# Part 1's mixture in 18 chunks of 256 tokens at 192 bytes from the weights, not 12 blocks of 384

## The chip, the core and the metric

The kernel runs on one core of a Trainium2 chip. The metric is the device time of one execution in microseconds (us). The engines are named as the profile names them: PE (TensorE matmuls), PEld (TensorE's weight loads, which overlap PE), DVE (VectorE), ACT (ScalarE), POOL (GpSimd) and SP, whose queue issues most DMAs.

## The reference, cut to what matters

```python
B, H, S, D = 8, 8, 576, 64                      # attention; keys and values pooled by 8
k_p = k.reshape(B, H, S // 8, 8, D).mean(axis=3)
v_p = v.reshape(B, H, S // 8, 8, D).mean(axis=3)
attn = softmax(q @ k_p^T / sqrt(D))             # 72 scores for each token and head
x = (attn @ v_p).transpose(0, 2, 1, 3).reshape(4608, 512)
# Part 1's mixture, d_ff 768
h = np.maximum(np.maximum(x @ w1, x @ w2), x @ w3)
y = h @ w_out                                   # (4608, 512)
# Part 2, d_ff 2048
z = np.maximum(y @ w_in, 0.0)
out = z * z @ w_out2
```

All is float32. Each matmul operand is split in a high and a low half (`PARTS`: high·high, high·low, low·high), so one product of 128x128 weights takes three matmuls.

## The kernel before

**Part 1** takes 4608 tokens in 12 blocks of 384 (`T1`, `NB1`). `attention(j)` makes the x of block j, and `moe1(j)` the mixture on it. `moe1` is a generator of 22 steps (`STEPS`): for each of the 6 slices f of d_ff three steps e, each a group of 12 matmuls into one PSUM tile `ps` (three such tiles in `mm_ps`, shared by all steps); e = 0 is copied by ACT to `hm` (L547), e = 1 and 2 are joined by DVE's max (L549), and after e = 2 `split` makes h, the high half on ACT (L135) and the low on DVE (L136). Then come four output steps d, each a group of 18 matmuls over the six h, copied by ACT to `ys` (L566) and stored by a DMA from ACT's queue to `y_dram` (L567). `x` lies in eight buffers, h in six, two more (`ah_p`) serve the first two slices of block 1.

**The order** is written out by hand. Every load, softmax, transpose, value product and mixture step is put in `todo` with a due time, in units of one step; `run` sorts them. Step i of block j is due at `j * STEPS + i`; the first six steps of block 1 are due among the output steps of block 0. Attention for block j is due about one block ahead, spread by `pace`. The weights of Part 1 are converted from 64 bit to two float32 halves on the chip (`convert`, `split`) during the first steps, and those of Part 2 (`load_second`, `prepare_in`, `prepare_out`) between block 2 and the last block (`SECOND`), with results parked in DRAM; the second of each pair of arrays combines rows first (L478, L507, four DVE operations).

**Placement.** The pools stand one behind another in SBUF: `const`, `w_p` (weights of Part 1), `x_p`, `h_p`, `t_p` from the left. A weight array is 4096 bytes for each partition, an x or h tile 3072, all multiples of 256, so x and h start at the same place as the weights modulo 256. `ah_p` lies elsewhere, at 128 modulo 256 from them. In Part 2 `leave(y_p, 192)` and two more such calls put the moving operand 192 bytes from the stationary one modulo 256, in both of its products.

**Part 2** takes 9 blocks of 512 tokens with matmuls of 128x256 (L701, L825), and reads y back from `y_dram` (`load_y`, L644), piecewise where a half of 256 tokens crosses a block of 384.

Of the kernel before, what the change touches and what calls it, by code (L numbers as in the profile page):

```python
# [32 lines left out]
NE = 3  # L33
T1 = 384
NB1 = NT // T1
T2 = 512
NB2 = NT // T2

# [4 lines left out]


STEPS = NE * KF1 + KD

# [15 lines left out]
AHEAD = 2  # L64
BRISK = 0.7

SECOND = (2, NB1 - 1)


NATURAL = 1  # L70
# [25 lines left out]
def attention_moe_kernel(ctx: ExitStack, tc: tile.TileContext, q, k, v, vn, w1, w2, w3, wo1, wi2, wo2, out):  # L96
# [20 lines left out]
        (m, g, h): dram.tile([P, 2, 2, 256], F32, name=f"wo2_dram{m}_{g}_{h}")  # L117
        for m in range(1, 8) for g in range(2) for h in range(2)
    }
    y_dram = [dram.tile([KD, P, T1], F32, name=f"y_dram{j}") for j in range(NB1)]  # L120

# [55 lines left out]


    w_p = s1.enter_context(tc.tile_pool(name="w_p", bufs=1))
    x_p = s1.enter_context(tc.tile_pool(name="x_p", bufs=2 * KD))
    h_p = s1.enter_context(tc.tile_pool(name="h_p", bufs=KF1))
    t_p = s1.enter_context(tc.tile_pool(name="t_p", bufs=2))

    s_at = ctx.enter_context(ExitStack())
# [2 lines left out]
    sm_p = s_at.enter_context(tc.tile_pool(name="sm_p", bufs=4, side="right"))  # L189
    pt_p = s_at.enter_context(tc.tile_pool(name="pt_p", bufs=2, side="right"))  # L190
    xf_p = s_at.enter_context(tc.tile_pool(name="xf_p", bufs=1, side="right"))
    ah_p = s_at.enter_context(tc.tile_pool(name="ah_p", bufs=AHEAD, side="right"))
    sc_ps = s_at.enter_context(tc.tile_pool(name="sc_ps", bufs=2, space=PSUM))
    tr_ps = s_at.enter_context(tc.tile_pool(name="tr_ps", bufs=1, space=PSUM))
    av_ps = s_at.enter_context(tc.tile_pool(name="av_ps", bufs=1, space=PSUM))
# [8 lines left out]
    kbd = kv_p.tile([P, NPAIR, 2, SP], F32, name="kbd")  # L204
    nc.gpsimd.memset(kbd, 0.0)
    vst_f = []
    for _ in range(2):
        vf = t_p.tile([P, T1], F32, tag="ys", name="vst_f")[:SP].rearrange("s (p a d) -> s p a d", a=3, d=D)
        nc.gpsimd.memset(vf, 0.0)
        vst_f.append(vf)  # L210
    K_SCALE = 1.0 / (POOL * D**0.5)
# [80 lines left out]

    def attention(j):

        x_t[j] = [None] * NPAIR
        n_tiles = sum(NPAIR * len(score_tiles(n)) for _, _, n, _ in pieces(j))
        pace = (STEPS - 1) / n_tiles
        at = (j - 1) * STEPS + pace / 2 - (LAG_T + LAG_V + LEAD_X)
        brisk = BRISK if j == 1 else 1
        pace *= brisk  # L300
        if j > CARRIED and j % 3 == 1:
            at -= 1
            pace *= 0.88
        for b, s0, n, t in pieces(j):
            if s0 == 0 and b < NATURAL:
                tiles = []
                when = at - pace / 2 + LAG_T + LAG_V if t else at + pace / 2
                todo.append((when - LEAD_LOAD, lambda b=b, tiles=tiles: tiles.extend(load_natural(b))))
                todo.append((when, lambda tiles=tiles: pool_v(tiles)))
            for p in range(NPAIR):  # L310
                load, prepare, softmax, carry, transpose, values = attend(j, b, s0, n, p, t)
                todo.append((at - brisk * LEAD_LOAD, load))
                todo.append((at - brisk * LEAD_PREP, prepare))
                todo.append((at, softmax))
                late = 0
                if j >= CARRIED:
                    todo.append((at + LAG_C, carry))
                    late = 1
                todo.append((at + brisk * LAG_T + late, transpose))
                at += pace * len(score_tiles(n))  # L320
                todo.append((at - pace + brisk * (LAG_T + LAG_V) + late, values))
# [10 lines left out]
    def attend(j, b, s0, n, p, t):  # L332
# [56 lines left out]
        def transpose():  # L389
# [12 lines left out]
            for h in range(2):  # L402
# [13 lines left out]
                else:  # L416
                    nc.scalar.activation(pt[0][:, h, :n], tr, AF.Copy)

        def values():
            if t == 0:  # L420
                x_t[j][p] = x_p.tile([P, 2, T1], F32R, tag="x", name="x")
            x = x_t[j][p][:, :, t : t + n]
            if whole:
                av = av_ps.tile([P, T1], F32, tag="av0", name="av0")[:, :n]
                for h in range(2):
                    nc.tensor.matmul(
                        av, lhsT=vst_f[p // 2][:, p % 2, h : h + 2].rearrange("p a d -> p (a d)"), rhs=pt[0][:, h, :n],
                        start=(h == 0), stop=(h == 1),
                    )
                split(x, av)  # L430
                return
            hi, lo = pt[0][:, 0, :, :n], pt[0][:, 1, :, :n]
            xf = xf_p.tile([P, T1], F32, tag="xf", name="xf")[:, :n]
            for h in range(2):
                av = av_ps.tile([P, T1], F32, tag=f"av{h}", name=f"av{h}")[:, :n]
                lhsT = vst[:, p, 2 * h : 2 * h + 2].rearrange("p a d -> p (a d)")
                nc.tensor.matmul(av, lhsT=lhsT, rhs=hi[:, h], start=True, stop=False)  # L437
                nc.tensor.matmul(av, lhsT=lhsT, rhs=lo[:, h], start=False, stop=True)  # L438
                r, o = slice(h * D, (h + 1) * D), slice((1 - h) * D, (2 - h) * D)
                nc.scalar.activation(xf[r], av[o], AF.Copy)  # L440
                nc.vector.tensor_tensor(out=xf[r], in0=av[r], in1=xf[r], op=ALU.add)  # L441
            split(x, xf)

        return load, prepare, softmax, carry, transpose, values

# [82 lines left out]

    def moe1(j):

        x = x_t.pop(j)
        hs = []
        for f in range(KF1):
            hm = t_p.tile([P, T1], F32, tag="hm", name="hm")
            h = (ah_p if j == 1 and f < AHEAD else h_p).tile([P, 2, T1], F32R, tag="h", name="h")
            for e in range(NE):
                ps = mm_ps.tile([P, T1], F32, tag="ps", name="ps")
                n = 0
                for kk in range(KD):
                    for a, c in PARTS:  # L540
# [12 lines left out]
            hs.append(h)  # L553
            now[0] = hm
        for d in range(KD):
            ps = mm_ps.tile([P, T1], F32, tag="ps", name="ps")
            n = 0
            for kk in range(KF1):
                for a, c in PARTS:
                    nc.tensor.matmul(  # L560
                        ps, lhsT=wo1_t[kk][:, a, d * P : (d + 1) * P], rhs=hs[kk][:, c],
                        start=(n == 0), stop=(n == 3 * KF1 - 1),
                    )
                    n += 1
            ys = t_p.tile([P, T1], F32, tag="ys", name="ys")
            nc.scalar.activation(ys, ps, AF.Copy)  # L566
            nc.scalar.dma_start(out=y_dram[j][d], in_=ys)  # L567
            yield
# [6 lines left out]
    def add_moe1(j):  # L575
        steps = moe1(j)
        for i in range(STEPS):
            when = j * STEPS + i
            if j == 1 and i < NE * AHEAD:
                when = NE * KF1 + i * KD / (NE * AHEAD)  # L580
            todo.append((when, functools.partial(next, steps, None)))

    todo = []
# [3 lines left out]
            todo.append((0.9 * (NE * f + e) - 12, functools.partial(load_w1, f, e)))  # L587
    for kk in range(KF1):
        todo.append((0.9 * (NE * KF1 + kk) - 12, functools.partial(load_wo1, kk)))
    for j in range(NB1 - 1):  # L590
        add_moe1(j)
        attention(j + 1)

    second = []
    for f in range(0, KF2, 2):
# [39 lines left out]
    def load_y(j):  # L635

        for n, (r, h) in enumerate(((0, 0), (0, 1), (1, 0), (1, 1))):
            yr = shared_place(n, [P, 2, HT], "yr")
            for i in range(2):
                t = 0  # L640
                while t < HT:
                    b, o = divmod(j * T2 + h * HT + t, T1)
                    n = min(HT - t, T1 - o)
                    nc.sync.dma_start(out=yr[:, i, t : t + n], in_=y_dram[b][2 * r + i, :, o : o + n])  # L644
                    t += n
            yr_t[j, r, h] = yr

    def mix_y(j):
# [30 lines left out]
    early.append(functools.partial(fetch_in, 0, w2_p))  # L679
    early += [functools.partial(split_y, 0, m) for m in ORDER]  # L680
    for i, f in enumerate(early):
        todo.append(((NB1 - 1) * STEPS + (i + 0.5) * (NE * KF1) / len(early), f))
    add_moe1(NB1 - 1)
    run()
    s1.close()
    g_p = ctx.enter_context(tc.tile_pool(name="g_p", bufs=4, reuse_waits="tile"))
# [214 lines left out]
```

## Time and profile before

| | |
|---|---|
| time, median of 3 runs | 1459.99 us (1458.57 to 1462.32) |
| the profiled execution's own time | 1462.14 us |
| its span in the trace | 1459.7 us |
| Part 1's last matmul, Part 2's first | 749.3 us |
| PE, PEld busy | 98%, 96% of the span |
| DVE, ACT, POOL busy | 67%, 52%, 13% |

The span is what the trace covers, from the first instruction to the last; the execution's own time is 2.4 us longer. Busy shares are means over stages that differ, so a stage is read by itself.

### The profile page before, as it was taken

The page shows a single profiled execution, that of the slowest core. Times are in us where ns is not written, and L with a number is a line of the kernel's source. Part 1 is how long each engine was busy: PE and PEld are TensorE (multiplying, and loading weights), DVE is VectorE, ACT ScalarE, POOL GpSimd, SP SyncE. Part 2 cuts the span into 40 slices and gives each one's busy share as a digit, 9 for nine tenths or more (in the row PEclk, how much of TensorE's full clock was granted, in tenths as well). Part 3 has the DMA queues.
Part 4 walks back from the last instruction along what each step waited for, and adds up shares of the span by engine and source line. Part 5 has one row for each costly group of instructions (what it writes and reads, how often), then busy time and mean ns, then how long its engine had stood idle before and what let it go on. Part 6 is the DMA issues. An engine that isn't in the chain of part 4 may idle for free.

```text
span 1459.7 us, 27670 instructions
## 1 busy us (share of the span) xinstructions
PE 1425.5 (98%) x10410; PEld 1403.0 (96%) x10410; DVE 977.9 (67%) x1754; ACT 759.4 (52%) x1959; POOL 182.9 (13%) x229
## 2 busy tenths in 40 slices
PE   6889999999999999999999999999999999999998
PEld 4879999999999999999999999999999999999998
DVE  5887477656675756646336767686867767686865
ACT  7795366655665657655223544453535444454543
POOL 3441022212322222221000000000000000000000
PEclk9989999999999999999999999999999999999999
DMA  7554145444455444433459747566566666555746
GB/s 226 182 169 141 62 143 180 162 140 142 146 180 177 149 148 142 133 120 107 167 190 355 290 160 256 186 223 222 209 221 224 232 231 221 204 217 199 258 153 209
DMA packets 125029, 272.81 MB, mean 187 GB/s; under 512 B 13504, under 2 KB 69568, under 8 KB 124896
## 3 DMA queue, kind: packets, MB, share of 16 engines
q1 hardware_dynamic: 117984, 261.61, 52.8%
q10 hardware_dynamic: 6912, 9.44, 1.8%
q8 instruction: 82, 1.34, 0.4%
q14 instruction: 51, 0.42, 0.1%
HBM read 213.91 MB, written 48.23 MB: 180 GB/s over the span
## 4 chain that ended last, share of the span: by engine, by line
PE 77%; DMA 5%; DVE 2%; ACT 1%; issue 1%; SPq 0%; POOL 0%; ACTq 0%; DVEq 0%; POOLq 0%
PE ps L701 23%; PE ps L541 22%; PE ps L560 8%; PE accB L825 6%; PE accA L825 6%; PE accE L825 3%; PE accF L825 3%; DMA wo2s<-wo_dram 3%; PE accD L825 2%; PE sc L367 2%; PE av L438 1%; PE av L437 1%; DMA wraw<-in_wi_dram 0%; PE tr L408 0%; DMA yr<-y_dram 0%
## 5 line engine op out<-in xcount | busy, mean ns | idle before, releaser
L541 PE MATMUL ps<-x,w 128*128 128x384 f32 x2592 | 491.0, 342 | 5.5 <-ACT w L135 3.0
L541 PEld LDWEIGHTS ps<-x,w 128*128 128x128 f32 x2592 | 452.0, 190 | 8.3 <-ACT w L135 3.4
L701 PE MATMUL ps<-y,wi2s 128*128 128x256 f32 x3024 | 372.8, 278 | 0.7 <-DVE a L672 0.2
L701 PEld LDWEIGHTS ps<-y,wi2s 128*128 128x128 f32 x3024 | 357.2, 188 | 2.4 <-DVE c L672 1.3
L560 PE MATMUL ps<-h,wo 128*128 128x384 f32 x864 | 159.0, 337 | 0.1
L560 PEld LDWEIGHTS ps<-h,wo 128*128 128x128 f32 x864 | 149.6, 188 | 0.3 <-ACT wo L135 0.2
L714 ACT ACTIVATE c<-c 128x512 f32<-128x512 f32 x90 | 56.3, 626 | 168.6 <-DVE c L672 168.0
L672 DVE TENSOR_TENSOR c<-ps,c 128x512 f32<-128x512 f32 x144 | 98.2, 687 | 66.4 <-PE ps L701 63.5
L549 DVE TENSOR_TENSOR hm<-ps,hm 128x384 f32<-128x384 f32 x144 | 79.7, 553 | 81.3 <-PE ps L541 78.8
L135 ACT ACTIVATE g<-c 128x512 fp32r<-128x512 f32 x144 | 90.3, 627 | 57.0 <-DVE c L711 23.3
L825 PE MATMUL accA<-wo2s,g 128*128 128x256 f32 x864 | 115.6, 277 | 0.0
L825 PE MATMUL accB<-wo2s,g 128*128 128x256 f32 x864 | 111.7, 279 | 3.9 <-DMA wo2s<-wo_dram 3.0
L372 ACT ACTIVATE ss<-sc,st 128x72 f32<-128x72 f32 (+1 forms) x320 | 97.8, 320 | 29.9 <-DVE st L369 24.8
L825 PEld LDWEIGHTS accB<-wo2s,g 128*128 128x128 f32 x864 | 104.5, 189 | 4.9 <-ACT g L135 2.2
L136 DVE TENSOR_TENSOR g<-c,g 128x512 fp32r<-128x512 f32 x144 | 97.8, 686 | 16.4 <-ACT g L135 16.4
L825 PEld LDWEIGHTS accA<-wo2s,g 128*128 128x128 f32 x864 | 107.0, 188 | 0.0
L441 DVE TENSOR_TENSOR xf<-av,xf 64x192 f32<-64x192 f32 (+1 forms) x112 | 50.7, 452 | 39.3 <-ACT xf L440 37.6
L378 POOL TENSOR_TENSOR ss<-ss,st 128x432 f32<-128x432 f32 (+1 forms) x64 | 53.1, 830 | 178.3 <-DVE st L377 95.0
L135 ACT ACTIVATE h<-hm 128x384 fp32r<-128x384 f32 x72 | 37.6, 522 | 56.2 <-DVE hm L549 55.5
L372 ACT ACTIVATION_READ_ACCUMULATOR ss<-sc,st 128x1 f32 (+1 forms) x320 | 66.2, 207 | 0.0
L135 ACT ACTIVATE g<-s 128x512 fp32r<-128x512 f32 x72 | 44.3, 630 | 35.3 <-DVE s L675 17.5
L163 ACT ACTIVATE wraw<-wraw 128x512 int32<-128x512 uint32 x56 | 37.8, 675 | 43.4 <-DMA wraw<-in_wi_dram 16.4
(111 smaller groups left out, 1929.2 us busy)
## 6 DMA issues: line engine op xcount, KB each, us to landing
wo2s<-wo_dram SPq DMA_DIRECT2D x252, 512.0 KB, 5.8
wi2s<-wi_dram SPq DMA_DIRECT2D x24, 512.0 KB, 6.5
wraw<-in_wo_dram SPq DMA_DIRECT2D x22, 512.0 KB, 3.9
wraw<-in_w_dram SPq DMA_DIRECT2D x18, 512.0 KB, 5.2
y_dram<-ys ACTq DMA_DIRECT2D x48, 192.0 KB, 2.7
wraw<-in_wi_dram SPq DMA_DIRECT2D x16, 512.0 KB, 3.7
wi_dram<-wraw SPq DMA_DIRECT2D x16, 512.0 KB, 3.0
wo_dram<-wraw SPq DMA_DIRECT2D x64, 128.0 KB, 2.1
```

Of the source, the lines that this page charges most:

```text
L135: nc.scalar.activation(hi, src, AF.Copy)
L136: engine.tensor_tensor(out=lo, in0=src, in1=as_f32(hi), op=ALU.subtract)
L372: nc.scalar.activation(ss[:, i, h], src[:, i, h], AF.Exp, bias=st[:, 0, i, h : h + 1], accum_out=st[:, 1, i, h : h + 1],)
L378: nc.gpsimd.tensor_tensor(out=ss, in0=ss, in1=st[:, 2].rearrange("p g (h o) -> p g h o", o=1).to_broadcast([m, g, 2, SP]), op=ALU.mult,)
L441: nc.vector.tensor_tensor(out=xf[r], in0=av[r], in1=xf[r], op=ALU.add)
L541: nc.tensor.matmul(ps, lhsT=w1_t[f, e][:, a, kk * P : (kk + 1) * P], rhs=x[kk][:, c], start=(n == 0), stop=(n == 3 * KD - 1),)
L549: nc.vector.tensor_tensor(out=hm, in0=ps, in1=hm, op=ALU.max)
L560: nc.tensor.matmul(ps, lhsT=wo1_t[kk][:, a, d * P : (d + 1) * P], rhs=hs[kk][:, c], start=(n == 0), stop=(n == 3 * KF1 - 1),)
L672: nc.vector.tensor_tensor(out=out, in0=in0, in1=in1, op=ALU.add)
L701: nc.tensor.matmul(bank[:, u * HT : (u + 1) * HT], lhsT=wi2_t[2 * gr + u][i][:, a, o + kk * P : o + (kk + 1) * P], rhs=y_t[j][m][:, c, kk] ...
L714: nc.scalar.activation(c, c, AF.Relu)
L825: nc.tensor.matmul(bank[:, i * 256 : (i + 1) * 256], lhsT=g[:, a, u * HT + i * P : u * HT + (i + 1) * P], rhs=w[:, u, c], start=(n == 0 an ...
```

## The change

Part 1's mixture works on 18 chunks (`CT`, `NC`) of 256 tokens, with matmuls of 256 columns. Attention still works in pieces of the 12 blocks; `to_x` splits each piece into the x tiles of the chunks it covers, in two parts where it crosses from one chunk to the next. x lies in 16 buffers of 2048 bytes (four chunks of four), put 192 bytes further by `leave(x_p, 192)`; h follows in eight. Step i of chunk c is due at `c * CHUNK + i * CT / T1`. The first six steps of chunk 1 are due from 6.3 on, one a unit, inside chunk 0; the second piece of block 1 (the first of batch 1) is five units later; attention for later blocks is due up to 7.3 units earlier and, for blocks 2 and 3, closer together. y is stored in chunks of 256, which are the halves that Part 2 reads.

```diff
+CT = 256
+NC = NT // CT
+CHUNK = STEPS * CT / T1
+FILL, FILL_PACE = 6.3, 1.0
+LATER = 5
-SECOND = (2, NB1 - 1)
+SECOND = (2, (NC - 2) * CT / T1)
-    y_dram = [dram.tile([KD, P, T1], F32, name=f"y_dram{j}") for j in range(NB1)]
+    y_dram = [dram.tile([KD, P, CT], F32, name=f"y_dram{c}") for c in range(NC)]
-    x_p = s1.enter_context(tc.tile_pool(name="x_p", bufs=2 * KD))
-    h_p = s1.enter_context(tc.tile_pool(name="h_p", bufs=KF1))
+    x_p = s1.enter_context(tc.tile_pool(name="x_p", bufs=1))
+    leave(x_p, 192)
+    h_p = s1.enter_context(tc.tile_pool(name="h_p", bufs=KF1 + AHEAD))
-    ah_p = s_at.enter_context(tc.tile_pool(name="ah_p", bufs=AHEAD, side="right"))
...
         pace *= brisk
+        if j == 2:
+            at -= 2
+            pace *= 0.85
+        elif j > 2:
+            at -= CHUNK / 2
+            if j == 3:
+                pace *= 0.9
...
+            if j == 1 and s0 == 0:
+                at += LATER
...
+        def to_x(src):
+            u = 0
+            while u < n:
+                c, o = divmod(j * T1 + t + u, CT)
+                m = min(n - u, CT - o)
+                if o == 0:
+                    x_t[c, p] = x_p.tile([P, 2, CT], F32R, tag=f"x{c % 4}_{p}", name="x")
+                split(x_t[c, p][:, :, o : o + m], src[:, u : u + m])
+                u += m
...
-                split(x, av)
+                to_x(av)
-            split(x, xf)
+            to_x(xf)
...
     def moe1(j):
-            hm = t_p.tile([P, T1], F32, tag="hm", name="hm")
-            h = (ah_p if j == 1 and f < AHEAD else h_p).tile([P, 2, T1], F32R, tag="h", name="h")
+            hm = t_p.tile([P, CT], F32, tag="hm", name="hm")
+            h = h_p.tile([P, 2, CT], F32R, tag="h", name="h")
-                ps = mm_ps.tile([P, T1], F32, tag="ps", name="ps")
+                ps = mm_ps.tile([P, CT], F32, tag="ps", name="ps")
...
     def add_moe1(j):
-            when = j * STEPS + i
+            when = j * CHUNK + i * CT / T1
             if j == 1 and i < NE * AHEAD:
-                when = NE * KF1 + i * KD / (NE * AHEAD)
+                when = FILL + i * FILL_PACE
...
-                t = 0
-                while t < HT:
-                    b, o = divmod(j * T2 + h * HT + t, T1)
-                    n = min(HT - t, T1 - o)
-                    nc.sync.dma_start(out=yr[:, i, t : t + n], in_=y_dram[b][2 * r + i, :, o : o + n])
-                    t += n
+                nc.sync.dma_start(out=yr[:, i], in_=y_dram[2 * j + h][2 * r + i])
```

## Rows read from the trace of the kernel before

**Rows 1.** Busy time by stretch, with count, granted clock, DMA share and GB/s.
```profile
20.00:120.00 100.00, 85.33 (x456) 76.26 (x454) 85.78 (x165) 82.09 (x270) 47.20 (x38) 0.90 0.56 175
150.00:700.00 550.00, 548.84 (x3397) 545.49 (x3396) 346.05 (x715) 318.81 (x1017) 129.22 (x174) 1.00 0.45 145
840.00:1440.00 600.00, 597.38 (x5194) 594.71 (x5194) 432.98 (x687) 276.82 (x477) 0.00 (x0) 1.00 0.62 214
101.70:104.90 3.20, 3.20 (x11) 3.20 (x11) 1.55 (x2) 2.78 (x7) 2.75 (x3) 0.50 0.39 146
```

**Rows 2.** Timeline of PE: start and length in us, merged instructions and their count.
```profile
699.38 37.60 PE L541 MATMUL ps<-x,w 128*128 128x384 f32 x216
736.82 12.64 PE L560 MATMUL ps<-h,wo 128*128 128x384 f32 x72
...
863.86 6.76 PE L701 MATMUL ps<-y,wi2s 128*128 128x256 f32 x58
```

**Rows 3.** Groups of PE by line: count, busy us, mean ns of one, idle before.
```profile
L541 PE MATMUL ps<-x,w 128*128 128x384 f32 x2592 | 491.0, 342 | 5.5 <-ACT w L135 3.0 <-DVE x L136 1.2 <-DVE hm L549 0.8
L560 PE MATMUL ps<-h,wo 128*128 128x384 f32 x864 | 159.0, 337 | 0.1
L701 PE MATMUL ps<-y,wi2s 128*128 128x256 f32 x3024 | 372.8, 278 | 0.7 <-DVE a L672 0.2
```

**Rows 4.** Groups of ACT and DVE by line and shape, the same columns.
```profile
L549 DVE TENSOR_TENSOR hm<-ps,hm 128x384 f32<-128x384 f32 x144 | 79.7, 553 | 81.3 <-PE ps L541 78.8 <-POOL wsum L136 1.3
L441 DVE TENSOR_TENSOR xf<-av,xf 64x192 f32<-64x192 f32 x56 | 19.8, 353 | 14.6 <-ACT xf L440 13.8
L136 DVE TENSOR_TENSOR h<-hm,h 128x384 fp32r<-128x384 f32 x72 | 46.9, 651 | 15.2 <-ACT h L135 14.1
L547 ACT ACTIVATE hm<-ps 128x384 f32<-128x384 f32 x72 | 34.9, 485 | 24.2 <-PE ps L541 21.1 <-PE av L438 1.8 <-ACT ys L566 0.8
L440 ACT ACTIVATE xf<-av 64x192 f32<-64x192 f32 x56 | 18.2, 325 | 6.3 <-PE av L438 4.4 <-PE sc L367 0.6
L135 ACT ACTIVATE h<-hm 128x384 fp32r<-128x384 f32 x72 | 37.6, 522 | 56.2 <-DVE hm L549 55.5
L566 ACT ACTIVATE ys<-ps 128x384 f32<-128x384 f32 x48 | 23.3, 492 | 37.6 <-PE ps L560 26.4 <-DMA y_dram<-ys 11.1
L478 DVE TENSOR_TENSOR wsum<-wbits 128x256 f32<-128x256 f32 x16 | 6.1, 419 | 0.1
L372 ACT ACTIVATE ss<-sc,st 96x72 f32<-96x72 f32 x128 | 39.0, 313 | 17.0 <-DVE st L369 12.1 <-issue 4.6
```

**Rows 5.** Timeline of PE and DVE around one conversion of Part 2's weights.
```profile
326.44 5.57 PE L541 MATMUL ps<-x,w 128*128 128x384 f32 x31
327.52 1.32 DVE L164 SCALAR_TENSOR_TENSOR wbits<-wbits,wraw 128x512 int32<-128x512 int32 x1
328.87 0.69 DVE L167 SCALAR_TENSOR_TENSOR wbits<-wraw,wbits 128x512 int32<-128x512 int32 x1
...
331.64 0.56 DVE L549 TENSOR_TENSOR hm<-ps,hm 128x384 f32<-128x384 f32 x1
...
335.75 2.36 PE L541 MATMUL ps<-x,w 128*128 128x384 f32 x12 [0.78 <-DVE hm L549]
```

**Rows 6.** Timeline of all engines at one start of the output steps.
```profile
396.57 2.85 PE L560 MATMUL ps<-h,wo 128*128 128x384 f32 x15
...
397.45 0.55 DVE L549 TENSOR_TENSOR hm<-ps,hm 128x384 f32<-128x384 f32 x1
...
399.26 0.65 PE L367 MATMUL sc<-kbd,qr 128*96 128x144 f32 x4
399.44 0.52 ACT L135 ACTIVATE h<-hm 128x384 fp32r<-128x384 f32 x1
```

**Rows 7.** DMA issues by line: queue, count, KB each, median us to landing.
```profile
y_dram<-ys ACTq DMA_DIRECT2D x48, 192.0 KB, 2.7
yr<-y_dram SPq DMA_DIRECT2D x48, 128.0 KB, 5.9
```

More of the change, by code (lines that the diff above doesn't have):

```diff
@@ L206, in attention_moe_kernel @@
     vst_f = []
-    for _ in range(2):
-        vf = t_p.tile([P, T1], F32, tag="ys", name="vst_f")[:SP].rearrange("s (p a d) -> s p a d", a=3, d=D)
+    for i in range(2):
+        vf = x_p.tile([P, 2 * CT], F32, tag=f"x3_{i}", name="vst_f")[:SP, :T1].rearrange("s (p a d) -> s p a d", a=3, d=D)
         nc.gpsimd.memset(vf, 0.0)
@@ L293, in attention @@
     def attention(j):
-        x_t[j] = [None] * NPAIR
         n_tiles = sum(NPAIR * len(score_tiles(n)) for _, _, n, _ in pieces(j))
@@ L417, in transpose @@
                     nc.scalar.activation(pt[0][:, h, :n], tr, AF.Copy)
+        def to_x(src):
[7 more added lines that the diff above has]
+                u += m
         def values():
-            if t == 0:
-                x_t[j][p] = x_p.tile([P, 2, T1], F32R, tag="x", name="x")
-            x = x_t[j][p][:, :, t : t + n]
             if whole:
@@ L529, in moe1 @@
     def moe1(j):
-        x = x_t.pop(j)
+        x = [x_t.pop((j, p)) for p in range(NPAIR)]
         hs = []
         for f in range(KF1):
-            hm = t_p.tile([P, T1], F32, tag="hm", name="hm")
-            h = (ah_p if j == 1 and f < AHEAD else h_p).tile([P, 2, T1], F32R, tag="h", name="h")
+            hm = t_p.tile([P, CT], F32, tag="hm", name="hm")
+            h = h_p.tile([P, 2, CT], F32R, tag="h", name="h")
             for e in range(NE):
-                ps = mm_ps.tile([P, T1], F32, tag="ps", name="ps")
+                ps = mm_ps.tile([P, CT], F32, tag="ps", name="ps")
                 n = 0
@@ L555, in moe1 @@
         for d in range(KD):
-            ps = mm_ps.tile([P, T1], F32, tag="ps", name="ps")
+            ps = mm_ps.tile([P, CT], F32, tag="ps", name="ps")
             n = 0
@@ L564, in moe1 @@
                     n += 1
-            ys = t_p.tile([P, T1], F32, tag="ys", name="ys")
+            ys = t_p.tile([P, CT], F32, tag="ys", name="ys")
             nc.scalar.activation(ys, ps, AF.Copy)
@@ L589, in attention_moe_kernel @@
         todo.append((0.9 * (NE * KF1 + kk) - 12, functools.partial(load_wo1, kk)))
-    for j in range(NB1 - 1):
-        add_moe1(j)
-        attention(j + 1)
+    for j in range(1, NB1):
+        attention(j)
+    for c in range(NC - 2):
+        add_moe1(c)
     second = []
@@ L681, in attention_moe_kernel @@
     for i, f in enumerate(early):
-        todo.append(((NB1 - 1) * STEPS + (i + 0.5) * (NE * KF1) / len(early), f))
-    add_moe1(NB1 - 1)
+        todo.append(((NC - 2) * CHUNK + (i + 0.5) * (NE * KF1) / len(early), f))
+    add_moe1(NC - 2)
+    add_moe1(NC - 1)
     run()
```

## The prediction

> **What bounds the kernel now.** I read the busy times by stretch first, then the timeline of PE, then the groups of instructions with what they waited for. The reader should see in [rows 1] that PE is busy 548.8 of 550 us between 150 and 700 us at the full granted clock, while DVE and ACT are busy 346 and 319: in the steady part of Part 1 nothing but PE sets the end, and a change is worth what it takes from PE or what it makes PE wait. Between 20 and 120 us it is different: PE is busy 85.3 of 100 us at a mean granted clock of 0.90, with DVE at 85.8 and ACT at 82.1. There the weights of Part 1 are still being converted, and the engines that do it are nearly full.
>
> What one matmul costs I take from long unbroken rows of PE's timeline, where a row's length less one matmul's own duration [rows 3], over the count less one, is the distance between starts. Part 1: (37.60 - 0.34) / 215 = 173.3 ns for the first product and (12.64 - 0.34) / 71 = 173.2 ns for the second, both at 384 columns; Part 2: (6.76 - 0.28) / 57 = 113.7 ns at 256 columns [rows 2]. For each column that is 0.451 ns against 0.444. Part 2 already has 256 columns and the 192 bytes between its operands; Part 1 has 384 columns and its operands at the same place modulo 256.
>
> **The change part by part.**
>
> *Matmuls.* The number goes from 12 x 288 = 3456 to 18 x 288 = 5184, the columns stay. Before: 3456 x 173.3 = 598.9 us. After, at Part 2's clean distance: 5184 x 113.7 = 589.4 us, a gain of 9.5 us. The other end comes from Part 2 as a whole, where 5194 matmuls took 597.4 us of busy PE, 115.0 ns each [rows 1]: 596.2 us, a gain of 2.7 us. I take the clean value, because the value before is a clean one too and Part 1 in its steady part has hardly a wait of its own: all of L541 idled 5.5 us and L560 0.1 us [rows 3].
>
> A fixed toll on each matmul would turn this round. At the half clock 11 matmuls of 384 start within 3.20 us [rows 1], at most 320 ns from start to start (3.20 / 10), and half of that is 160: at the full clock 13.3 ns of the 173.3 do not shrink with the clock. If each matmul kept these 13.3 ns whatever its width, 256 columns would take 160 x 2/3 + 13.3 = 120.0 ns and the chunks 622.1 us, 23 us more than now. Part 2's 113.7 ns at the same width speaks against it. The Trainium skill, "TensorE: Matmul & The Clock Gate", section "Back-to-back issue gap", gives a gap of N / 2.4 + 2.5 ns when warm, so a fixed part for each matmul: 162.5 and 109.2 ns, an estimate of 561.6 us before and 566.1 after, 4.5 us more instead of 9.5 less. The trace disagrees with both figures (173.3 and 113.7 ns) and with their ratio.
>
> *Evictions and splits.* From [rows 4] a column costs DVE (553 - 353) / 192 = 1.04 ns and ACT (485 - 325) / 192 = 0.83 ns, so at 256 columns L547 takes about 378 ns, L566 385, the two halves of h 415 and 518, L549 420. ACT: 12 x (6 x 485 + 6 x 522 + 4 x 492) = 96.1 us becomes 18 x (6 x 378 + 6 x 415 + 4 x 385) = 113.4. DVE: 12 x (12 x 553 + 6 x 651) = 126.5 becomes 18 x (12 x 420 + 6 x 518) = 146.7. `to_x` cuts a piece at 12 of the 17 inner chunk ends, for four pairs each: 48 more splits, at the fixed parts 522 - 384 x 0.83 = 203 ns on ACT and 651 - 384 x 1.04 = 252 on DVE, 10 and 12 us. In all ACT gets 27 us more and DVE 32. Their idle time in the steady stretch, 231 and 204 us [rows 1], hides it as work. It costs nothing as long as no single piece comes late.
>
> *Late evictions.* Three `ps` tiles serve all steps, so a group's result must be out within the two groups behind it. That is now 24 x 173.3 = 4.16 us and becomes 24 x 113.7 = 2.73 us, plus what attention puts between. [rows 5] shows the case that fills it: DVE converts and combines weights from 327.5, the max between them comes at 331.64, and the group at 335.75 waits 0.78 us for another late max. A combining conversion takes DVE 0.7 + 0.7 + 4 x 0.42 = 3.1 us [rows 4, 5], with the max behind it 3.5; there are 16 of these (L478's count of `wsum`). In the worst case each stalls PE for 3.5 - 2.73 = 0.8 us, 13 us together; at best attention's matmuls and the mixed order of DVE cover it, 0. The second place is the start of the output steps: h of slice 5 must be there after 15 matmuls, 2.60 us now and 1.71 after. In [rows 6] the high half is done at 399.96, 3.39 us behind the start at 396.57; with 0.65 us of attention in between that would stall about 1.0 us. At worst all 18 chunks pay it, 18 us; at best none. Behind a waiting max on DVE stand the softmax and value steps of attention, which PE needs three units later, so a late piece does not spread at once. I take 4 us for both places: one conversion in 16 stalled PE visibly so far, which is nearer to 0 than to 31.
>
> *y.* ACT's queue issues 72 stores of 128 KB instead of 48 of 192; `ys` has two buffers, and ACT has idled 11.1 us for a store to land [rows 4]. A store takes 2.7 us [rows 7] and two output groups will take 36 x 113.7 = 4.1 us, so the buffer is free in time; if a store takes over 4 us, ACT and the evictions behind it wait. SP issues 72 loads of y in Part 2 instead of 96. Both lie beside other work: 0, within 1 us either way.
>
> *Start.* Each array of w1 feeds a group of 1.36 us instead of 2.08, so while the 18 arrays are converted PE has 13 us less to do; six steps of chunk 1 (72 matmuls, 8.2 us) are moved in among them, out of the output steps where such steps stood before. Against it the first piece of batch 1 stands five units later, with 16 exponentials of 0.31 us on ACT alone [rows 4], 5 us and more that no longer stand before the weights. Loss at worst 13 us, gain at most the 14.7 us that PE idles there [rows 1]. The two ends are equally far and I take 0.
>
> *Conversions.* `SECOND` ends at 10.67 instead of 11, so they come 4% denser; the earlier due times of attention answer to chunks that begin in the middle of a block. 0 for both, under the same bounds as the late evictions.
>
> Sum: 1462.1 - 9.5 + 4 + 0 = 1456.6 for the profiled execution, which stood 2.1 above the median of the runs; against the median of 1460.0 that is **1454.5 us**.
>
> **The rivals.** *The slack eats the gain.* PE starts to wait on L549, L547 and L566 at many places and gives back 6 to 14 us: for it speaks that evictions were over 3 us late already [rows 5, 6]; against it that L541 waited 0.8 us for them in all [rows 3]. Time 1456 to 1464, no change that counts.
>
> *Late results decide (slower).* If each combining conversion and each start of output steps costs what its worst case gives, 13 + 18 = 31 us go against 9.5: 1460 + 21.5 = 1481; the point from which it is slower than before is 9.5 us of stalls, about a third of that; half of the worst gives 1466. For and against it as above; ACT's and DVE's load rises by 27 and 32 us.
>
> *The toll stays (slower).* Part 1 keeps 13.3 ns on each matmul, 120.0 ns at 256 columns: 1460 + 23 + 4 = 1487. Only a difference between the products of the two parts that the rows do not show could do this. The Trainium skill's rule named above is this rival in a milder form.
>
> *The start gains.* The delayed piece lets the weights through, PE fills up earlier and wins 5 to 10 of its 14.7 idle us, and stalls stay at 2: 1460 - 9.5 + 2 - 7.5 = 1445.
>
> That the 192 bytes are not reached I rule out: the tiles ahead of x and h are multiples of 256 bytes after the one of 192.
>
> **How the numbers follow.** Forecast (1451 to 1456) 0.36, slack eats the gain 0.24, late results 0.16, toll 0.05, start gains 0.19. A measurement of this kernel tells about 0.3% from no change, 4.4 us, so under 1455.6 is faster: 0.36 + 0.19 = 0.55; within 0.24; slower 0.16 + 0.05 = 0.21. The range runs from the start's gain less 2 us for the unknown of y (1443) to half of the late results' worst case with a bad start of 4 us (1470), which leaves the toll and the upper half of the late results out.
>
> **What would show it.** Right: unbroken rows of L541 with 113 to 114 ns from start to start; PE busy over 99% from 150 us on; Part 1's last matmul some 5 us before 749. Wrong: a distance near 120 (the toll); idle time of PE behind L549, L547 or L135 of more than 9 us (late results); PE busy under 80 us between 20 and 120 (the start).

## The result and the profile after

The changed kernel is slower: 1474.91 us, median of 4 runs (1474.51 to 1477.53), against 1460.25 us for the kernel before in the runs beside it. The ratio is 1.0104, with a 95% interval of 1.0086 to 1.0121. The forecast was 1454.5 us; the time lies above its range. The profiled execution took 1474.51 us, with a span of 1472.4.

In the kernel after, L541 has become L562 (first product), L560 L581 (second product), L549 L570 (DVE's max), L547 L568, L566 L587, L135 and L136 L141 and L142, and L701 L719. First the busy times by stretch of the kernel after, which answer [rows 1]:

```profile
20.00:120.00 100.00, 79.77 (x484) 71.89 (x485) 79.93 (x169) 78.40 (x268) 45.42 (x38) 0.80 0.54 173
150.00:700.00 550.00, 548.73 (x4760) 547.25 (x4759) 359.18 (x839) 329.70 (x1124) 124.40 (x173) 1.00 0.46 150
840.00:1440.00 600.00, 597.00 (x5211) 595.79 (x5210) 436.93 (x693) 275.11 (x474) 0.00 (x0) 1.00 0.62 217
```

From 150 us on PE is as full as before (548.7 of 550 us). Between 20 and 120 us it is busy 79.8 us, where it was 85.3, at a mean granted clock of 0.80, where it was 0.90. PE's timeline, which answers [rows 2], tells when Part 1 ends and how far its matmuls stand apart:

```profile
272.34 5.61 PE L562 MATMUL ps<-x,w 128*128 128x256 f32 x48
...
297.52 3.00 PE L562 MATMUL ps<-x,w 128*128 128x256 f32 x24
...
312.42 2.99 PE L562 MATMUL ps<-x,w 128*128 128x256 f32 x24
...
696.34 24.64 PE L562 MATMUL ps<-x,w 128*128 128x256 f32 x216
720.82 8.32 PE L581 MATMUL ps<-h,wo 128*128 128x256 f32 x72
...
761.62 2.99 PE L719 MATMUL ps<-y,wi2s 128*128 128x256 f32 x24
```

Part 2 begins at 761.6 us instead of 749.3. These 12.3 us are nearly the whole difference of the two spans (1472.4 - 1459.7 = 12.7), so Part 2 plays no part in it. As in the prediction, a row's length less one matmul's duration (0.284 us, the mean of L562), over the count less one, is the distance from start to start. The last rows give (24.64 - 0.284) / 215 = 113.3 ns and 113.2, as forecast. But the rows at 297.5 and 312.4 give 118.1 and 117.7, at the full clock and with no wait. A row of 48 some 25 us earlier gives 113.3. The single starts in the trace show that these are no sums of a few pauses: they stand 113 to 114 ns apart all through the row at 272.3, 117 to 120 all through the other two. So the same matmul has two paces here.

What was done by when is seen in the busy times of a line alone, from the start of the span to 120 us: of the kernel after for L562 and L581,

```profile
0.00:120.00 120.00, 49.01 (x288) 43.61 (x288) 0.83 0.58 189
0.00:120.00 120.00, 4.87 (x41) 4.76 (x42) 0.83 0.58 189
```

and of the kernel before for L541 and L560:

```profile
0.00:120.00 120.00, 57.28 (x252) 48.34 (x252) 0.91 0.59 188
0.00:120.00 120.00, 7.54 (x34) 5.73 (x34) 0.91 0.59 188
```

By 120 us the kernel before has issued 252 + 34 = 286 matmuls of 384 columns, the kernel after 288 + 41 = 329 of 256, which is 219.3 of 384. It is 66.7 of them behind, and 66.7 x 173.3 ns = 11.6 us: almost the whole loss arises here. Behind 120 us, 3170 matmuls took 749.3 - 120 = 629.3 us before, attention between them included: 198.5 ns for each 384 columns. After, 4855 (3236.7 of 384) took 641.6 us: 198.2 ns. At the forecast 113.7 ns these 4855 should have saved 4855 x (173.3 x 2/3 - 113.7) = 8.9 us, 2.8 ns of that pace. They saved about a tenth of it. The second pace accounts for most of the rest: of the 4696 distances between neighbouring mixture matmuls that the trace holds behind 120 us, 2719 are 112 to 115 ns and 1739 are 116 to 119, and 1739 x 4.4 = 7.7 us.

PE's waits, over the whole kernel (engine, line, what it waited for; total, times, longest):

```profile
PE sc L381 <- ACT kbd L250: 7.5, 2, 6.5
PE accB L843 <- DMA wo2s<-wo_dram: 5.2, 6, 3.0
PE sc L381 <- ACT ss L386: 4.4, 4, 3.1
PE ps L562 <- ACT x L141: 3.6, 2, 2.2
PE tr L422 <- POOL ss L392: 3.4, 3, 2.1
PE ps L562 <- DVE x L142: 3.3, 3, 1.2
PE av L447 <- DVE x L142: 2.7, 2, 1.8
...
PE ps L562 <- DVE hm L570: 1.0, 1, 1.0
PE ps L581 <- ACT ys L587: 0.8, 1, 0.8
PE ps L581 <- DVE hm L570: 0.7, 1, 0.7
```

The late evictions, L570 and L587, cost 1.0 + 0.8 + 0.7 us. Between 120 and 740 us the mixture waited 0.8 us for L587 and 0.4 for h and for nothing else, against 0.8 for L549 in the kernel before. The wait for `wo2s` lies in Part 2. The other large ones are attention's own and the mixture's for x, and they lie before 120 us. The groups of ACT and DVE that answer [rows 4]:

```profile
L570 DVE TENSOR_TENSOR hm<-ps,hm 128x256 f32<-128x256 f32 x216 | 90.5, 419 | 83.9 <-PE ps L562 76.9 <-ACT hm L568 3.2 <-PE tr L422 1.6
L142 DVE TENSOR_TENSOR h<-hm,h 128x256 fp32r<-128x256 f32 x108 | 49.9, 462 | 24.2 <-ACT h L141 23.4
L141 ACT ACTIVATE h<-hm 128x256 fp32r<-128x256 f32 x108 | 44.9, 416 | 81.8 <-DVE hm L570 81.3
L568 ACT ACTIVATE hm<-ps 128x256 f32<-128x256 f32 x108 | 40.9, 381 | 21.4 <-PE ps L562 19.3 <-ACT ys L587 0.8 <-PE av L459 0.4
```

How a cut piece passes between the engines is seen in the timeline of the kernel after, around one piece of chunks 0 and 1:

```profile
40.42 0.36 ACT L141 ACTIVATE x<-av 128x256 fp32r<-128x256 f32 x1
40.55 2.20 DVE L170 SCALAR_TENSOR_TENSOR wbits<-wbits,wraw 128x512 int32<-128x512 int32 x1 [1.60 <-ACT wbits L168]
...
42.67 0.41 DVE L142 TENSOR_TENSOR x<-av,x 128x256 fp32r<-128x256 f32 x1
...
43.12 0.28 ACT L141 ACTIVATE x<-av 128x128 fp32r<-128x128 f32 x1 [0.99 <-DVE x L142]
...
43.14 1.65 PE L562 MATMUL ps<-x,w 128*128 128x256 f32 x6 [0.97 <-DVE x L142]
...
44.87 0.28 DVE L142 TENSOR_TENSOR x<-av,x 128x128 fp32r<-128x128 f32 x1
```

One piece takes four steps in turn, ACT, DVE, ACT, DVE, from 40.4 to 45.2 us: ACT waits 0.99 us for DVE, DVE is held by a conversion of weights, and PE waits 0.97 us for the low half. Last, POOL's timeline where the conversions of Part 1's weights end, after and before:

```profile
112.11 1.30 POOL L142 TENSOR_TENSOR wo<-wbits,wo 128x512 fp32r<-128x512 f32 x1
117.68 1.29 POOL L142 TENSOR_TENSOR wo<-wbits,wo 128x512 fp32r<-128x512 f32 x1 [4.26 <-ACT wo L141]
```

```profile
117.37 1.31 POOL L136 TENSOR_TENSOR wo<-wbits,wo 128x512 fp32r<-128x512 f32 x1 [2.24 <-ACT wo L135]
```

The last output weights are ready at 119.0 us after and at 118.7 before. The change has not moved this end, though the five arrays ahead of it come 2 to 5 us earlier.

### The profile page after: what moved, and what is told of

The parts are those of the page before. It is cut to its first block, busy times and chain, and to the rows that moved or that the text cites. A ratio compares the mean times of both kernels' runs of the same rounds, so it can differ in the third digit from the quotient of the medians.

```text
span 1472.4 us, 31593 instructions
## 1 busy us (share of the span) xinstructions
PE 1430.5 (97%) x12138; PEld 1412.2 (96%) x12138; DVE 991.9 (67%) x1910; ACT 773.3 (53%) x2103; POOL 177.3 (12%) x229
## 4 chain that ended last, share of the span: by engine, by line
PE 85%; DMA 6%; ACT 4%; DVE 3%; issue 1%; POOL 0%; SPq 0%; ACTq 0%; DVEq 0%; POOLq 0%
PE ps L562 27%; PE ps L719 23%; PE ps L581 9%; PE accB L843 6%; PE accA L843 6%; PE accF L843 3%; PE accE L843 3%; DMA wo2s<-wo_dram 3%; PE accD L843 2%; PE sc L381 2%; ACT ss L386 1%; DMA wraw<-in_w_dram 1%; PE av L458 1%; PE av L459 1%; DMA vr<-in_v_dram 1%
## 5 line engine op out<-in xcount | busy, mean ns | idle before, releaser
L562 PE MATMUL ps<-x,w 128*128 128x256 f32 x3888 | 491.8, 284 | 8.1 <-ACT x L141 3.6
L562 PEld LDWEIGHTS ps<-x,w 128*128 128x128 f32 x3888 | 470.0, 191 | 10.8 <-DVE x L142 4.2
L719 PE MATMUL ps<-y,wi2s 128*128 128x256 f32 x3024 | 373.0, 277 | 1.1 <-ACT c L753 0.7
L719 PEld LDWEIGHTS ps<-y,wi2s 128*128 128x128 f32 x3024 | 357.3, 188 | 2.3 <-ACT c L753 1.3
L581 PE MATMUL ps<-h,wo 128*128 128x256 f32 x1296 | 160.9, 280 | 1.9 <-ACT ys L587 0.8
L581 PEld LDWEIGHTS ps<-h,wo 128*128 128x128 f32 x1296 | 154.4, 188 | 2.5 <-ACT ys L587 0.9
L570 DVE TENSOR_TENSOR hm<-ps,hm 128x256 f32<-128x256 f32 x216 | 90.5, 419 | 83.9 <-PE ps L562 76.9
L141 ACT ACTIVATE g<-c 128x512 fp32r<-128x512 f32 x144 | 90.2, 627 | 59.3 <-DVE c L729 23.3
L142 DVE TENSOR_TENSOR g<-c,g 128x512 fp32r<-128x512 f32 x144 | 97.9, 687 | 17.0 <-ACT g L141 17.0
L141 ACT ACTIVATE h<-hm 128x256 fp32r<-128x256 f32 x108 | 44.9, 416 | 81.8 <-DVE hm L570 81.3
L142 DVE TENSOR_TENSOR h<-hm,h 128x256 fp32r<-128x256 f32 x108 | 49.9, 462 | 24.2 <-ACT h L141 23.4
L141 ACT ACTIVATE g<-s 128x512 fp32r<-128x512 f32 x72 | 44.4, 630 | 35.8 <-DVE s L692 15.9
```

The source lines that it names most:

```text
L141: nc.scalar.activation(hi, src, AF.Copy)
L142: engine.tensor_tensor(out=lo, in0=src, in1=as_f32(hi), op=ALU.subtract)
L562: nc.tensor.matmul(ps, lhsT=w1_t[f, e][:, a, kk * P : (kk + 1) * P], rhs=x[kk][:, c], start=(n == 0), stop=(n == 3 * KD - 1),)
L570: nc.vector.tensor_tensor(out=hm, in0=ps, in1=hm, op=ALU.max)
L581: nc.tensor.matmul(ps, lhsT=wo1_t[kk][:, a, d * P : (d + 1) * P], rhs=hs[kk][:, c], start=(n == 0), stop=(n == 3 * KF1 - 1),)
L719: nc.tensor.matmul(bank[:, u * HT : (u + 1) * HT], lhsT=wi2_t[2 * gr + u][i][:, a, o + kk * P : o + (kk + 1) * P], rhs=y_t[j][m][:, c, kk] ...
```

## The experiments

Two questions were open: what sets the distance of the matmuls, and what loses 11.6 us before 120 us. In the table, the mixture done by 120 us is counted as above, in matmuls of 384 columns; the pace is the time from 120 us to Part 2's first matmul over what was left of the mixture in the same unit, attention included. Ratios are to the kernel before, run beside each; its median was 1459.4 to 1464.0 us in these groups of runs, so differences of a few us between medians of different groups say little. The three kernels with the short conversion compute with other values than the weights.

| kernel | median, us | ratio (95%) | done by 120 us | Part 2 begins, us | pace, ns |
|---|---|---|---|---|---|
| before | 1460.25 | | 286 | 749.3 | 198.5 |
| after | 1474.91 | 1.0104 (1.0086 to 1.0121) | 219 | 761.6 | 198.2 |
| 384 at 192 bytes | 1466.07 | 1.0021 (1.0007 to 1.0035) | 291 | 750.9 | 199.3 |
| 384 at 64 | 1463.54 | 1.0001 (0.999 to 1.0013) | 288 | 748.6 | 198.4 |
| 256 at 0 | 1494.66 | 1.0214 (1.0197 to 1.0231) | 218 | 782.4 | 204.6 |
| 256 at 64 | 1485.6 | 1.0149 (1.0131 to 1.0166) | 224 | 771.9 | 201.7 |
| 256 at 128 | 1490.56 | 1.0217 (1.019 to 1.0245) | 225 | 777.8 | 203.6 |
| nine fill steps | 1480.97 | 1.0126 (1.0096 to 1.0157) | 211 | 770.4 | 200.4 |
| fill from 2.0 | 1484.12 | 1.0163 (1.0137 to 1.019) | 201 | 770.6 | 199.9 |
| piece not later | 1478.76 | 1.01 (1.0075 to 1.0125) | 231 | 765.0 | 200.0 |
| high halves first | 1475.64 | 1.0114 (1.0093 to 1.0134) | 222 | 762.0 | 198.5 |
| first chunk twice | 1492.45 | 1.0226 (1.0205 to 1.0247) | 313 | 779.7 | 200.7 |
| before, short conversion | 1454.07 | 0.9928 (0.9907 to 0.995) | 328 | 742.0 | 198.9 |
| after, short conversion | 1463.8 | 1.0006 (0.999 to 1.0021) | 289 | 751.2 | 199.3 |
| after, short, high halves first | 1462.98 | 0.9989 (0.9978 to 1.0001) | 307 | 748.9 | 199.7 |

**The placement alone, in the kernel before.**

```diff
     x_p = s1.enter_context(tc.tile_pool(name="x_p", bufs=2 * KD))
+    leave(x_p, 192)
```

> The kernel before with its blocks of 384 and only the placement of the change: x and h start 192 bytes further, modulo 256, from the weights. Theory P (placement sets the distance between matmuls, width only scales it): the unbroken rows of L542 fall from 173.3 ns to 1.5 x 113.4 = 170.1 ns or less, 3456 x 3.2 = 11 us, 1449 us. Rival W (the lower cost of a column comes from the width alone): the distance stays at 173.3 ns and the time at 1460 us.

Nothing is gained; the ratio of 1.0021 is even a small loss. The last unbroken row of the first product is the same to the last digit as the one in [rows 2], but an earlier one is not. Here is one of 45 at 192 bytes with the last one, and then the same 45 in the kernel before:

```profile
269.83 8.13 PE L542 MATMUL ps<-x,w 128*128 128x384 f32 x45
...
700.93 37.60 PE L542 MATMUL ps<-x,w 128*128 128x384 f32 x216
```

```profile
270.60 7.99 PE L541 MATMUL ps<-x,w 128*128 128x384 f32 x45
```

That is 173.3 ns at 384 columns in the last row, with 192 bytes as with 0, and 177.0 against 173.8 in the earlier one. So 192 bytes bring a second pace at 384 columns too: 1057 of the 3023 distances behind 120 us are 175 to 179 ns there, and 264 of 3028 in the kernel before.

**The width alone, in the kernel after.**

```diff
-    leave(x_p, 192)
```

> The changed kernel without the 192 bytes: chunks of 256, x and h at the same place as the weights modulo 256. Theory P: the 13.3 ns above 160 at 384 columns belong to this place and stay, so 120 ns from start to start, 5184 x 4.8 = 25 us more than the 115.2 ns now: 1500 us. Rival W: the distances stay at 113 to 114 and 117 to 118 ns, 1475 us.

Part 2 begins 20.8 us later than with the 192 bytes (782.4 against 761.6), while the mixture done by 120 us is the same. It is all in the distance:

```profile
713.27 26.08 PE L561 MATMUL ps<-x,w 128*128 128x256 f32 x216
739.19 8.80 PE L580 MATMUL ps<-h,wo 128*128 128x256 f32 x72
```

(26.08 - 0.284) / 215 = 120.0 ns, and 119.9 for the second product: the value of the toll, 13.3 ns on 160 x 2/3. So with both operands at the same place the toll is the same at the two widths tried, and the 192 bytes take away part of it at 256 columns. At 384 columns they take away nothing. Theory P is right here and was wrong at 384 columns; for rival W it is the other way round.

**Other distances at 256 columns, and one more at 384.**

```diff
-    leave(x_p, 192)
+    leave(x_p, 128)
```

> The changed kernel with 128 bytes between x, h and the weights, not 192. Theory M (the place sets the distance from a few fixed rates, as 120.0 at 0 bytes and 113.4 or 117.7 at 192): one of these rates or another fixed one, the same over long rows. At 384 columns 128 bytes were 3 ns dearer than 0, so I expect no rate under 117 ns: 1480 to 1495 us. Rival (any place but 0 does): 113.4 and 117.7 as at 192, 1475 us.

```diff
-    leave(x_p, 192)
+    leave(x_p, 64)
```

> The changed kernel with 64 bytes between x, h and the weights, not 192. Theory M (the place picks one of a few fixed distances; so far 120.0 at 0 bytes, 113.4 or 117.7 at 192, 115 to 123 mixed at 128): long rows at one or two fixed distances again; if only 113.4 occurs, the steady part wins 9 us and the time is 1466 us, if it is 117.7 or more, 1485 us. I expect the latter, since the shift from 192 to 128 made it dearer.

```diff
     x_p = s1.enter_context(tc.tile_pool(name="x_p", bufs=2 * KD))
+    leave(x_p, 64)
```

> The kernel before with 64 bytes between x, h and the weights in blocks of 384. Theory M: another fixed distance than 173.3 ns, as 384 columns at 192 bytes had 173.3 and 177 and at 128 bytes up to 180; I expect no less than 173.3: 1460 to 1466 us. If it is 170 or less, 1449 us, a version better than both kernels.

The last stretch without attention, at 128 bytes and 256 columns, at 64 and 256, and at 64 and 384:

```profile
709.43 25.79 PE L562 MATMUL ps<-x,w 128*128 128x256 f32 x216
```

```profile
704.01 25.60 PE L562 MATMUL ps<-x,w 128*128 128x256 f32 x216
```

```profile
698.62 37.60 PE L542 MATMUL ps<-x,w 128*128 128x384 f32 x216
```

They give 118.6, 117.7 and 173.3 ns. At 128 bytes this is a mean: the single starts stand 114 to 123 ns apart, so theory M's fixed distance is not there, though the time lies in its range. At 64 bytes the pace is the second one of 192, and the time is the 1485 us expected. Of the four places 192 bytes is the best at 256 columns. At 384 none of the three tried goes below 173.3 ns, and 64 bytes give the time of before.

**Ways to fill PE earlier.** Nine steps of chunk 1 ahead of the output steps instead of six (one more tile for h), the same six from 2.0 on, and the delayed piece put back.

```diff
-AHEAD = 2
+AHEAD = 3
...
-    h_p = s1.enter_context(tc.tile_pool(name="h_p", bufs=KF1 + AHEAD))
+    h_p = s1.enter_context(tc.tile_pool(name="h_p", bufs=KF1 + AHEAD - 1))
...
+    ah_p = s_at.enter_context(tc.tile_pool(name="ah_p", bufs=1, side="right"))
...
-            h = h_p.tile([P, 2, CT], F32R, tag="h", name="h")
+            h = (ah_p if j == 1 and f == 2 else h_p).tile([P, 2, CT], F32R, tag="h", name="h")
```

> The changed kernel with nine steps of chunk 1, not six, among those of chunk 0 (one h tile more, its first use at another place). Theory C (a chunk gives PE too little work for each weight array while the arrays are converted): three steps of 12 x 113.5 ns more are done by the time the last array is ready, 4 us less, 1471 us. Rival D (the new due times of attention hold PE up): no change, 1475 us.

```diff
-FILL, FILL_PACE = 6.3, 1.0
+FILL, FILL_PACE = 2.0, 1.0
```

> The changed kernel with the six steps of chunk 1 due from 2.0 on, not 6.3. Theory K: they run where PE idles most, the half clock shrinks, 3 to 6 us less, 1470 us. Theory L: they stand in PE's order behind the same late x and queues and change nothing, or hold chunk 0 up: 1475 to 1478 us.

```diff
-LATER = 5
+LATER = 0
```

> The changed kernel with the first piece of batch 1 at its old due time (LATER = 0). Theory C: ACT and DVE get the piece's work back ahead of the weights, which come later, and PE loses up to 5 us more: 1475 to 1480 us. Rival D (the piece that was put later is what holds PE up): the start wins back most of its 13 us, 1463 to 1468 us.

None of the three regains the loss. With the nine steps and with the early six PE does less by 120 us (211 and 201 instead of 219), and the early six take 1484 us, longer than either theory asked. Without the delay PE does more (231), but then it waits 4.7 us in all between 120 and 740 us instead of 1.2, and the ratio stays (1.01 against 1.0104). The last output weights come earlier without the delay, at 115.1 us instead of 119.0:

```profile
113.79 1.30 POOL L142 TENSOR_TENSOR wo<-wbits,wo 128x512 fp32r<-128x512 f32 x1 [1.45 <-ACT wo L141]
```

Theory C's time came true, but not for its reason, that the weights would come later. The nine steps also show the second pace at its plainest, at the same distance of operands modulo 256 and with no attention between:

```profile
702.73 25.47 PE L563 MATMUL ps<-x,w 128*128 128x256 f32 x216
728.04 8.64 PE L582 MATMUL ps<-h,wo 128*128 128x256 f32 x72
736.52 25.60 PE L563 MATMUL ps<-x,w 128*128 128x256 f32 x216
```

These give 117.1, 117.7 and 117.7 ns, where the kernel after ran at 113.3. The first row holds both paces: its starts stand 113 to 114 ns apart up to 711.9 us and 117 to 119 from 714.3 on, with distances of up to 226 ns in the 2 us between. (The profiled execution of this kernel took 1489.0 us, 8 above its median.)

**The high halves of a cut piece first.** Both ACT operations of a piece are issued ahead of both DVE operations, so the piece no longer passes back and forth.

```diff
             while u < n:
...
-                split(x_t[c, p][:, :, o : o + m], src[:, u : u + m])
+                parts.append((x_t[c, p][:, :, o : o + m], src[:, u : u + m]))
                 u += m
+            for x, s in parts:
+                nc.scalar.activation(x[:, 0], s, AF.Copy)
+            for x, s in parts:
+                nc.vector.tensor_tensor(out=x[:, 1], in0=s, in1=as_f32(x[:, 0]), op=ALU.subtract)
```

> The changed kernel; where a piece crosses a chunk's end, both high halves are made first and then both low ones, not high, low, high, low. Theory L (the two cuts hand over between ACT and DVE three times instead of once, each time behind conversions, so the last x of block 0 comes at 54 instead of 46 us and the first full step with it): the start wins 3 to 5 us, 1470 us. Rival K (the late x does not matter, PE is idle because a chunk holds too little work for each array): 1475 us, the half clock between 20 and 120 us stays near 41 us.

The ratio does not change (1.0114). The mixture is further on at first: by 100 us it has 267 matmuls of 256 columns instead of 210. But by 120 us it has 288 + 45 = 333 instead of 329. PE's waits between 80 and 120 us tell why:

```profile
PE ps L586 <- POOL wo L142: 3.3, 3, 2.2
PE ps L567 <- POOL w L142: 2.7, 3, 1.4
PE ps L567 <- ACT w L141: 1.9, 2, 1.3
```

PE now waits for the weights. 333 is also all that the order lets it do before the last output weights, which come at 121.3 us here: 216 matmuls of chunk 0, the 72 of the six steps of chunk 1, and 45 of the output steps (by the code the first 15 of three groups, since there are three `ps`). The kernel before has the same 333 on its list, of 384 columns, and had done 286. So rival K's time came true; its half clock did not stay, as PE's row between 20 and 120 us shows (the clock is the last figure but two):

```profile
20.00:120.00 100.00, 78.64 (x504) 70.56 (x503) 84.93 (x175) 80.95 (x280) 49.27 (x37) 0.86 0.54 173
```

**More work for each array of weights.** The groups of chunk 0 are issued twice: 216 matmuls more, 216 x 113.3 = 24.5 us of work that the reference doesn't need.

```diff
-                n = 0
-                for kk in range(KD):
+                for _ in range(2 if j == 0 else 1):
+                    n = 0
+                    for kk in range(KD):
...
```

> The changed kernel with each group of 12 matmuls in the first product of chunk 0 issued twice into the same PSUM tile (the second starts over, so the values stay): 216 matmuls or 24.5 us of PE more. Theory K (while the arrays are converted PE's time is free, and its idling drops the clock): the half clock between 20 and 120 us falls from 41 towards 20 us and the time rises by under 8 us, to at most 1483. Rival (PE is the bound in the start too): 24 us more, 1499 us.

By 120 us 469 matmuls are done instead of 329, 140 more or 15.9 us of work: that much of the 24.5 us went into time that PE had to spare by then. The time still rises by 17.5 us (1492.45 - 1474.91), between the two expectations. Part 2 begins 18.1 us later; 10.0 of these are the 76 matmuls more that are left at 120 us, and 8.0 the slower pace behind it (200.7 against 198.2).

**The conversions shortened.** In both kernels the conversion of Part 1's weights stops behind its first operation, so that PE works on other values.

```diff
-    def convert(raw_pool, raw, after=None):
+    def convert(raw_pool, raw, after=None, short=False):
...
+        if short:
+            return as_f32(a)
...
-        split(w, convert(raw_pool, load_raw(raw_pool, src)), nc.gpsimd)
+        split(w, convert(raw_pool, load_raw(raw_pool, src), short=True), nc.gpsimd)
```

> The kernel before without the second ACT and both DVE operations of each conversion of Part 1's 24 weight arrays (their values are not the weights then): 16 us of ACT and 36 us of DVE less in the start. Theory K (while the arrays are converted PE has too little mixture to do, and the narrower chunk loses by that): the start shrinks by some 8 us, 1452 us, and the distance to the changed kernel with the same cut falls from 15 us to under 5. Rival S (the start loses for another reason, the order of attention in it): the distance stays 12 to 15 us.

> The changed kernel with the same operations left out of the conversions of Part 1's weights. Theory K: its start gains 10 us more than that of the kernel before, to within 5 us of it, about 1456 us. Rival S: 12 to 15 us above the kernel before with the same cut, about 1466 us.

The last output weights now come at 82.4 us (before) and 79.1 (after). The distance of the two kernels falls from 14.7 us (1474.91 - 1460.25) to 9.7 (1463.8 - 1454.07), and the mixture that the changed kernel is behind at 120 us from 66.7 matmuls to 328 - 289.3 = 38.7, or 6.7 us. Theory K misses: the distance is not under 5 us. Rival S misses by the medians, but by the ratios the distance is 11 us (1.0006 - 0.9928), and their intervals do not rule out its 12. By the count at 120 us the conversions carry some 5 us of the difference, not nearly all of it and not nothing.

**Both changes together.** The kernel after with the short conversion and with the high halves first; its edits are the two diffs above.

> The kernel after with Part 1's weights converted by their first ACT operation alone (their values are not the weights then, as in the run before it) and, beside that, each attention piece split with both of its high halves on ACT ahead of both low halves on DVE, so that a piece cut by a chunk's end no longer passes back and forth between the two engines. Theory L (what is left of the start's loss once the conversions are short is the late x of the cut pieces): PE's loss to 120 us falls from 33.6 us to within 3 us of the 25.4 of the kernel before with the same short conversion, and the time from 1463.8 to about 1457. Rival A (what is left comes from the attention work that stands in the start in another order, and from groups that give PE a third less to do for each array of weights): the loss stays at 31 to 35 us and the time between 1462 and 1466, x being earlier without PE having more to do.

The changed kernel is now 328 - 306.7 = 21.3 matmuls behind at 120 us, 3.7 us instead of 6.7. Part 2 begins 2.3 us earlier (748.9 instead of 751.2). The ratio goes from 1.0006 to 0.9989, 2.5 us by the kernels before, though the two intervals overlap. By the counts of the two traces late x costs about 3 us once the weights no longer hold PE. Neither theory is right as a whole. PE's idle time and the clock that was not granted, taken together to 120 us, fall from 34 to 26 us (19.3 of them idle time), the 26 of the kernel before with the short conversion, as theory L asked and the rival did not; the time stays within the rival's bounds. This run also shows the pace change with no attention between:

```profile
681.40 25.26 PE L569 MATMUL ps<-x,w 128*128 128x256 f32 x216
706.50 8.64 PE L588 MATMUL ps<-h,wo 128*128 128x256 f32 x72
```

In the first row the starts stand 112 to 115 ns apart, then comes one distance of 197 ns at 692.5 us, and from there on they stand 115 to 120 apart, 117.8 on the average, to the end of Part 1.

## Why the prediction was wrong

Two terms failed: the start, by 11.6 us, and the matmuls, whose gain of 9.5 us came to about 0.9.

**The start** is the step that failed most. It was taken as 0, between a loss of 13 us and a gain of 14.7; it is a loss of 11.6, near the bad end. The loss had been worked out in the right way, 0.72 us less work for PE with each of 18 arrays, and was then set against an idle time that the change cannot reach. The experiments show why:

- Until the last output weights are there, PE has one chunk, six steps of the next and the first parts of three output groups to do. That list is 333 matmuls in both kernels, and in 256 columns it is 222 of 384, less than the 286 that the kernel before had done. Even with x earlier PE reached 333 and no more. The six steps of chunk 1 that were counted as new work there stood on the list before. The list is a bound and not the whole cause: the nine fill steps lengthen it to 369, and PE had done 316 of them. A longer list with x earlier was not run.
- The end of the conversions did not come earlier (119.0 and 118.7 us), so the gain that was to come from the delayed piece did not exist; undoing the delay alone brought that end to 115.1 us and left the ratio at 1.01.
- Of the 11.6 us, 4.9 go when the conversions are short, and 3.0 more when the cut pieces are also split with the high halves first. Where the last 3.7 arise is open: the smaller work of each group and attention's order in the start are both left, and no run puts back the earlier due times of blocks 2 and later.

The lower clock is a companion of this, not its cause: with the high halves first the mean granted clock between 20 and 120 us was 0.86 instead of 0.80, and the time was the same.

**The matmuls** were forecast to gain 9.5 us, and behind 120 us the gain that was left of it, 8.9 us, came to about a tenth. The distance of 113.7 ns is real (113.3 in clean rows) but it is one of two. Beside it stands 117.7, which in this order costs most of what the narrower rows save (7.7 of 8.9 us). The step that failed here is the choice of one clean row as the pace of the whole part. The other end of the term, 2.7 us from Part 2 as a whole, was closer. What was called a comparison of 0.451 with 0.444 ns for each column mixed two effects: at 256 columns at the same place the distance is 120.0 ns, and the 192 bytes only make good what the width costs. The toll of that rival thus exists where both operands lie at the same place, which this change leaves; the rival did not name the place as the reason. It was given 0.05 because Part 2's 113.7 was read as the price of a width, and it is the price of a width and a place.

The Trainium skill, "TensorE: Matmul & The Clock Gate", section "Back-to-back issue gap", gives N / 2.4 + 2.5 ns as the gap of an isolated matmul, 109.2 ns at 256, and says that a stream with a weight load for each matmul departs from it; the prediction held the formula against such a stream. No run here shows 109.2 ns: the same width took 113.3, 117.7, 118.6 or 120.0 ns, by the place of the operands.

**Late evictions** were put at 4 us, with 31 as the worst. They cost 2.5 us over the whole kernel, and all waits of the mixture behind 120 us come to 1.2, so the rival that forecast a slower kernel was right on the sign for a reason that did not occur. The durations forecast were right: 419, 381, 379 and 416 ns against 420, 378, 385 and 415; only the low half of h took 462 instead of 518.

**y and the conversions of Part 2** were 0, and stayed so: Part 2 takes the same time from its first matmul on (710.8 us after, 710.4 before), and the waits between 120 and 740 us are the 1.2 us above.

Of the three signs set down ahead, the first (113 to 114 ns) held in part of the rows, PE was over 99% busy from 150 us on as said, and yet Part 1 ended 12.3 us later instead of 5 earlier. The sign named for a bad start, PE busy under 80 us between 20 and 120, is the one that showed: 79.8.

No kernel tried here that computes the reference's values beats the one before. The best, 384 columns at 64 bytes, equals it (1.0001).

## What to carry to other kernels

Where PE waits for weights that are still being made, count what it *can* do until they are there, not how long it idles: tiles of fewer tokens make that list shorter, and no order of the same list makes it longer. A longer list need not help either, as the nine fill steps show. A distance between matmuls belongs to a width and a placement together, so a value taken from another part of the kernel holds only if both agree; and a stretch where other matmuls are mixed in must be read for itself, since its pace may differ from the clean row. A term that lies between two far ends of opposite sign deserves a look for what excludes one of them before the middle is taken.

## What the runs showed of the hardware

- The distance at full clock with one weight load for each matmul, by columns and by the bytes between moving and stationary operand modulo 256: 384 columns 173.3 ns at 0 and 64, and 173.3 or 177 at 192; 256 columns 120.0 at 0, 117.7 at 64, 118.6 at 128 as the mean of 114 to 123, and 113.3 or 117.7 at 192. The weights stayed where they are in all of these, so no run tells the distance between the operands from the moving operand's own place modulo 256.
- At 192 bytes and 256 columns the pace can change where a few matmuls of attention are put between (113.3 in the row at 272.3 us, 118.1 at 297.5, 117.7 at 312.4) or behind a single longer distance (197 ns at 692.5 us with both changes together), and then a whole stretch of 216 can keep either one, as the rows of the kernel after and of the nine fill steps show at the same place in the program. What decides between the two was not found.
